# Scores two units ahead in a sparse attention, and a weight's chunks decoded into two separate places

## The chip, the core and the metric

The kernel runs on one core of a Trainium2 chip. The metric is device time in microseconds from the start to the end of one execution; of several executions the median counts. Times inside an execution come from the hardware profiler: PE is the matrix engine (its weight loads are listed apart, as PEld), DVE the vector engine, ACT the scalar engine, POOL the engine for general work, SP the engine whose queue issues most transfers. A queue (SPq, ACTq, POOLq) is the engine's sequencer, which issues DMAs and waits.

## What is computed

Block-sparse attention, followed by a token mix. The attention (batch 4, 8 heads, 768 positions, head width 64) works in 24 blocks of 32 positions. A block of queries sees its own block and both neighbours, the first and the last block, and three blocks drawn at random; the first and the last block see everything.

```python
scores = scale * np.matmul(q, k.transpose(0, 1, 3, 2))
...
scores = np.where(mask, scores, -1000000000.0)
scores = scores - np.max(scores, axis=-1, keepdims=True)
attn = np.exp(scores)
attn = attn / (np.sum(attn, axis=-1, keepdims=True) + 1e-09)
x = np.matmul(attn, v)
...
theta = x @ w_theta
zr, zi = x * np.cos(theta), x * np.sin(theta)
y = np.einsum('ts,bsd->btd', w_tok_r, zr) + np.einsum('ts,bsd->btd', w_tok_i, zi)
u = x + y
out = u + np.maximum(u @ w_ch, 0.0)
```

The weights arrive as 64-bit words and are decoded on the chip into a high and a low part.

## The kernel before

**Units and steps.** The attention has 56 units, 28 for each of two pairs of batches ("pair" 0 and 1). The first six of a pair are edge units (named "w"): the first and the last block of queries against a third of all keys each. The other 22 are inner units, one block of queries each, against 8 gathered blocks of keys. The order of the work is written out by hand: `attention` has one loop over steps n (from line 491), in which each engine gets its instructions in program order. Nothing reorders them, so an instruction that waits holds up all that stand behind it on its engine.

**A unit's chain.** `scores` (line 321): PE multiplies queries and keys into S (line 340, for edge units line 332), and DVE reduces S to the row minima m (line 343; the queries were scaled by -0.125). `weights` (353): four exponentials on ACT make P (line 360). `turn` (364): eight transpositions on PE make T (line 370). `evict` (372): two copies on ACT take T to pT (line 376). `values` (379): PE multiplies pT with the values into X (line 394). `finish` (405): DVE divides by the row sums (lines 401 to 403, or 417), and `store` writes the result to a scratch tensor xs.

**Buffers.** S has two places of two banks, by the unit's parity. T has two banks, both used by each unit. X, P, pT and m have two each; the gathered keys kg and the windows of values va have two, the gathered values vb four.

**One step before.** In step n the order is: decoder's Abs of a new piece (ACT); scores of n+1; a share of the block tables; register loads for n+4; window and sampled keys of n+3 copied into kg (POOL, lines 298 and 277); up to two decoding shares (DVE); turn of n; values of n-1; evict of n; weights of n+1; the third sampled block of n+3 copied (ACT, line 280); queries of n+3 scaled (ACT, line 247); the decoder's copy of the high part (ACT, line 81); finish of n-1; queries of n+6 loaded (SP); values of n+2 gathered (POOL, an indirect DMA, line 314); the window of values of n+1 loaded (SP, line 310), for two units of three after a copy from the other buffer (POOL, line 307); the store of n-1. Keys of pair 1 are loaded in odd steps 5 to 27, two blocks at a time (SP, line 232); its edge queries qe in step 24 (SP, line 258), and they are scaled on ACT in step 25 (line 247).

**Decoding.** A `Piece` is 512 or 576 columns of a weight. It is loaded into one of two raw buffers (line 59, on ACT's queue) and decoded in three shares on DVE: `bits` (lines 68 to 70), `rest` (lines 76 and 78), `low` (lines 85 and 86), with Abs (63) and the high copy (81) on ACT. The loop computes in `due` how many of the shares should be done by step n. Eight "early" pieces (theta and the first half of tok_r) are spread over steps 4 to 28, ten "late" ones (the second half of tok_r, the first two thirds of tok_i) over steps 29 to 52; at most two shares are done in a step. The late ones go to a tile `w_second` that takes the place in which pair 0 had its keys and values, 13824 columns under one tag. What is left of tok_i, and w_ch, are decoded in the token mix.

**The token mix** (`token_mix`, a generator) is advanced by `next(follow)` in the last six steps and then runs to the end: theta, sine and cosine, and the products with tok_r and tok_i (line 672), which are all PE-heavy.

Of the kernel before, what the change touches and what calls it, by code (L numbers as in the profile page):

```python
# [10 lines left out]
F32 = mybir.dt.float32  # L11
F32R = mybir.dt.float32r
# [168 lines left out]
        nc.vector.tensor_scalar(rows[0:96], base, ZEROS, None, op0=ALU.add)  # L181


def attention(tc, qT, qE, kT, vr, sampled, xs, ident, early_pieces, late_pieces, first_place, follow, spares):

# [13 lines left out]
    with ExitStack() as ctx, ExitStack() as early:  # L199
# [20 lines left out]
        def make_places(bp):  # L220

            if bp == 0:
                place = first_place([P, 13824], F32, "kv0")
                k = place[:, 0:6144]
                wide[bp] = [place[:, 6144 + 1040 * c : 6144 + 1040 * (c + 1)] for c in range(6)]
            else:
                k = kp.tile([P, 6144], F32, name="k1")
                wide[bp] = vbs + vbs[:2]
            ks[bp] = k.rearrange("r (s g f) -> r s g f", s=NB, g=8)
# [91 lines left out]
        def scores(unit):  # L321

            bp, i, x = unit
            s = st[unit] = {}
            sc = ps_s[units.index(unit) % 2].tile([P, 2, 2, 256], F32, tag="S", name=f"S{name(unit)}")
            heads = [(b, p, e) for b in range(2) for p in range(4) for e in range(2)]
            if i == "w":
                t, a = x
                q, keys = qes[bp], ks[bp][:, 8 * t : 8 * t + 8]
                for b, s_, e in [(b, p, e) for b, p, e in heads if p < 2]:  # L330
                    rows, p = slice(64 * e, 64 * e + 64), 2 * a + s_
                    nc.tensor.matmul(sc[64 * s_ : 64 * s_ + 64, e, b, :], q[rows, b, p, :], keys[rows, :, 4 * b + p, :], start=True, stop=True)
                if t == 0:
                    mxs[a] = wp.tile([P, 3, 4], F32, tag="mx", name=f"mx{name(unit)}")
                m = mxs[a][:, t]
            else:
                q, keys = qbs.pop((bp, i)), kgs[i % 2]
                for b, p, e in heads:
                    rows = slice(64 * e, 64 * e + 64)
                    nc.tensor.matmul(sc[32 * p : 32 * p + 32, e, b, :], q[rows, b, p, :], keys[rows, :, 4 * b + p, :], start=True, stop=True)  # L340
                m = wp.tile([P, 4], F32, tag="m", name=f"m{name(unit)}", bufs=2)

            nc.vector.tensor_reduce(m.rearrange("r (e b) -> r e b", e=2), sc, axis=AX.X, op=ALU.min)  # L343
# [118 lines left out]
        spares.append(lambda: qp.tile([P, 4, 4, 32], F32, tag="q", name=f"spare{len(spares)}", bufs=Q_BUFS))  # L462
        with tc.manual_schedule():
            load_edges(0)
# [22 lines left out]
            making = tab.make(nc, cp)  # L487
            next(making)
            do(0, weights)
            steps = len(units) + 1  # L490
            for n in range(steps):
                if n == len(units) - 1:
                    early_s.close()
                    next(follow)

                if n <= half:
                    due = 3 * len(early_pieces) * max(n - 3, 0) // (half - 3)
                else:

                    weight = lambda k: 4 * min(k, 6) + 7 * max(k - 6, 0)  # L500
                    due = 3 * len(early_pieces) + 3 * len(late_pieces) * weight(n - half) // weight(len(units) - 4 - half)
                due = min(due, 3 * len(decoder.pieces)) - decoder.at
                decoder.first_on_scalar(due)
                do(n + 1, scores)
                next(making, None)
                inner(n + 4, number_blocks)
                inner(n + 3, gather_window)
                inner(n + 3, gather_keys)
                if due > 0:
                    decoder.on_vector()  # L510
                if due > 1 and decoder.at % 3:
                    decoder.on_vector()
                do(n, turn)
                do(n - 1, values)
                if len(units) - 2 <= n < len(units):
                    next(follow)
                do(n, evict)
                do(n + 1, weights)
                inner(n + 3, gather_key)
                inner(n + 3, scale_q)  # L520
                decoder.on_scalar()
                do(n - 1, finish)
                if units[min(n + 6, steps - 2)][:2] not in ((0, 1), (0, 3)):
                    inner(n + 6, load_q)
                inner(n + 2, gather_values)

                inner(n + 1, lambda bp, i: load_window(bp, i) if i > 2 else None)
                inner(n + 3, lambda bp, i: load_window(bp, i) if i <= 2 else None)
                inner(n - 1, store)

                if n <= len(units) and units[n - 1][1:] in (("w", (2, 0)), ("w", (2, 1))):
                    joins.append(join(units[n - 1][0], units[n - 1][2][1]))
                if n % half > 6 and joins and next(joins[0], joins) is joins:
                    joins.pop(0)
# [12 lines left out]
                if len(units) - 6 <= n < len(units):  # L547
                    next(follow)
# [286 lines left out]
def sparse_attention_then_token_mix(ctx, tc, qT, qE, kT, vr, sampled, w_theta, w_tok_r, w_tok_i, w_ch, outT):  # L835
# [15 lines left out]

    def first_place(shape, dtype, name):
        return const.tile(shape, dtype, tag="place", name=name)

    rest = []

    def second():
        if not rest:  # L860
            rest.append(first_place([P, 2, 9 * 768], F32R, "w_second"))
        return rest[0]

    def tok(at):

        tile_, k = (first, at) if at < 3 else (second(), at - 3)
        return [tile_[:, x, 768 * k : 768 * k + 768] for x in range(2)]

    w["tok_r"] = tok
    w["tok_i"] = lambda j: tok(6 + j)  # L870
# [12 lines left out]

    def chunks(tile_, at, n):
        return lambda: [tile_()[:, x, 768 * at : 768 * (at + n)] for x in range(2)]

    early = pieces("theta", 0, 2048, 512, all_of("theta")) + pieces("tok_r", 0, 2304, 576, chunks(lambda: first, 0, 3))
    late = pieces("tok_r", 2304, 4608, 576, chunks(second, 0, 3)) + pieces("tok_i", 0, 3072, 512, chunks(second, 3, 4))

    def last():  # L890
        return pieces("tok_i", 3072, 4608, 256, chunks(second, 7, 2)) + pieces("ch", 0, 2048, 256, all_of("ch"))

    spares = []
    follow = token_mix(tc, w, last, xs, outT, bias, n_batch, lambda: spares[0]())
    attention(tc, qT, qE, kT, vr, sampled.bitcast(I32), xs, ident, early, late, first_place, follow, spares)
    for _ in follow:
        pass

# [46 lines left out]
```

## Time and profile before

| | us |
|---|---|
| median of 3 executions | 596.28 |
| the three executions | 595.65, 596.28, 603.92 |
| the profiled execution | 599.4 |
| its span, first to last instruction | 597.6 |
| PE busy (matmuls) | 548.1 |
| DVE busy | 423.8 |
| ACT busy | 335.6 |
| POOL busy | 180.8 |

How to read it: the profiled execution is a single one, 3.1 us above the median; its rows are compared with its own time. A row of stretches gives for each engine the busy time and, in brackets, the count of instructions. A row of waits reads "engine, what waited, <- what ended the wait: us in total, times, longest". In a timeline the columns are start, duration, engine, line, operation, output <- inputs, count, and in square brackets the idle time of the engine before it and what ended that. "issue" stands for idle time in which the engine waited for nothing that the profile shows. Durations of matmuls overlap, since they are pipelined. In a row of groups stand busy us and mean ns of one between the bars.

### The profile page before, as it was taken

The numbers are of one execution on the slowest core, as the hardware profiler recorded it, in microseconds if no ns is written. First come the engines' busy times: TensorE is split into PE (matmuls) and PEld (weight loads), VectorE is DVE, ScalarE is ACT, GpSimd is POOL, SyncE is SP. The second block draws the span as 40 slices with busy tenths as digits, with TensorE's granted clock in tenths as the row PEclk, the third lists the DMA queues.
The fourth block names the chain that finished last, engine by engine and source line by source line (L and its number), as shares of the span: only waits on it lengthen the run. The fifth ranks groups of instructions, "written<-read, shape, count | busy, mean of one in ns | idle before, by whom it ended". The sixth has DMA issues, their size and how long they took to land.

```text
span 597.6 us, 17323 instructions
## 1 busy us (share of the span) xinstructions
PE 548.1 (92%) x7092; PEld 436.6 (73%) x7092; DVE 423.8 (71%) x846; ACT 335.6 (56%) x684; POOL 180.8 (30%) x281
## 2 busy tenths in 40 slices
PE   6997886979967878999999999999999999999997
PEld 4765555556645545678888888888888888888886
DVE  3786876977889999968999996557732759613352
ACT  4797876758978866875565653344630445521220
POOL 1387957942687888530010010000000000000000
PEclk9898988979999998899999999999999999999999
DMA  8979889879988996852333132220212311102002
GB/s 313 353 216 263 249 254 258 233 199 318 282 242 236 238 251 184 207 159 73 94 84 104 43 89 88 89 62 10 71 36 79 95 39 34 37 27 81 1 1 105
DMA packets 53087, 86.67 MB, mean 145 GB/s; under 512 B 5392, under 2 KB 31632, under 8 KB 52624
## 3 DMA queue, kind: packets, MB, share of 16 engines
q1 hardware_dynamic: 43200, 53.28, 29.2%
q0 software_dynamic: 6944, 22.85, 14.4%
q10 hardware_dynamic: 2864, 9.44, 5.4%
q8 instruction: 56, 0.92, 0.7%
q14 instruction: 23, 0.19, 0.1%
HBM read 72.95 MB, written 12.58 MB: 143 GB/s over the span
## 4 chain that ended last, share of the span: by engine, by line
PE 36%; DVE 11%; ACT 5%; DMA 2%; issue 1%; DVEq 0%
PE ya L672 14%; PE yb L672 7%; PE o L697 2%; PE o L698 2%; PE o L699 2%; PE h L613 2%; PE h L616 2%; PE h L614 2%; ACT zh L654 2%; ACT t L623 1%; DVE rr L630 1%; DVE rr L629 1%; DVE xT L598 1%; DMA xa<-xs 1%; ACT t L622 1%
## 5 line engine op out<-in xcount | busy, mean ns | idle before, releaser
L672 PE MATMUL ya<-w_second,zh 128*128 128x512 f32 x288 | 106.9, 395 | 0.0
L672 PE MATMUL yb<-w_second,zh 128*128 128x256 f32 x288 | 80.2, 279 | 0.0
L360 ACT ACTIVATE P<-S,m 128x256 f32<-128x256 f32 x176 | 70.0, 499 | 14.9 <-DVE m L343 13.6
L370 PE MATMUL T<-ident,P 128*128 128x128 f32 x352 | 60.7, 301 | 10.0 <-ACT P L360 8.6
L370 PEld LDWEIGHTS T<-ident,P 128*128 128x128 f32 x352 | 41.7, 148 | 36.9 <-ACT P L360 29.6
L672 PEld LDWEIGHTS ya<-w_second,zh 128*128 128x128 f32 x288 | 54.1, 188 | 13.6
L343 DVE TENSOR_REDUCE m<-S 128x4 f32<-128x1024 f32 x44 | 53.6, 1217 | 10.2 <-PE S L340 9.0
L340 PE MATMUL S<-kg,q 64*32 64x256 f32 x1408 | 53.6, 390 | 7.2 <-issue 7.2
L394 PE MATMUL X<-vb,pT 128*32 128x65 f32 (+1 forms) x1408 | 50.4, 230 | 10.2 <-issue 10.1
L376 ACT COPY pT<-T 128x512 f32<-128x512 f32 x88 | 47.9, 601 | 19.4 <-PE T L370 18.9
L394 PE MATMUL X<-va,pT 128*32 128x65 f32 (+1 forms) x1408 | 50.4, 233 | 7.9 <-issue 5.4
L672 PE MATMUL ya<-w_second,zl 128*128 128x512 f32 x144 | 57.6, 400 | 0.0
L672 PEld LDWEIGHTS yb<-w_second,zh 128*128 128x128 f32 x288 | 54.3, 188 | 0.4
L314 POOL DMA_INDIRECT vb<-in_vr_dram,rows x44 | 46.1, 1047 | 20.3 <-PE X_w L394 8.6
L394 PEld LDWEIGHTS X<-va,pT 128*32 128x32 f32 (+1 forms) x1408 | 35.6, 116 | 16.7 <-issue 12.4
L394 PEld LDWEIGHTS X<-vb,pT 128*32 128x32 f32 (+1 forms) x1408 | 37.9, 117 | 12.2 <-issue 12.0
L705 DVE SCALAR_TENSOR_TENSOR of<-o,xT 128x512 f32<-128x512 f32 (+1 forms) x24 | 13.3, 557 | 46.0 <-PE o L699 42.5
L672 PE MATMUL yb<-w_second,zl 128*128 128x256 f32 x144 | 40.6, 282 | 0.0
L307 POOL COPY va<-va 32x1040 f32<-32x1040 f32 (+1 forms) x28 | 31.6, 1129 | 27.8 <-DMA va<-in_vr_dram 20.9
L613 PE MATMUL h<-w_theta_hi,xh 128*128 128x512 f32 x96 | 38.2, 398 | 0.4 <-ACT xh L602 0.4
L340 PEld LDWEIGHTS S<-kg,q 64*32 64x32 f32 x1408 | 23.0, 107 | 20.5 <-issue 11.7
L614 PE MATMUL h<-w_theta_lo,xh 128*128 128x512 f32 x96 | 37.9, 394 | 0.0
(169 smaller groups left out, 1309.2 us busy)
## 6 DMA issues: line engine op xcount, KB each, us to landing
va<-in_vr_dram SPq DMA_DIRECT2D x58, 130.0 KB
q<-in_qT_dram SPq DMA_DIRECT2D x22, 256.0 KB
xs<-xo SPq DMA_DIRECT2D x22, 256.0 KB
xr<-xs SPq DMA_DIRECT2D x22, 256.0 KB
xa<-xs SPq DMA_DIRECT2D x88, 64.0 KB
raw_tok_r<-in_w_tok_r_dram ACTq DMA_DIRECT2D x8, 576.0 KB
out_dram<-of SPq DMA_DIRECT2D x16, 256.0 KB
kv<-in_vr_dram SPq DMA_DIRECT2D x6, 520.0 KB
```

The costliest lines, as they stand in the source:

```text
L307: nc.gpsimd.tensor_copy(va[rows], vas[(i + 1) % 2][rows])
L314: nc.gpsimd.indirect_dma_start(out=vbs[(i + 1) % VB][rows], out_offset=None, in_=vr, in_offset=bass.IndirectOffsetOnAxis(ap=tab.rows[rows, ...
L340: nc.tensor.matmul(sc[32 * p : 32 * p + 32, e, b, :], q[rows, b, p, :], keys[rows, :, 4 * b + p, :], start=True, stop=True)
L343: nc.vector.tensor_reduce(m.rearrange("r (e b) -> r e b", e=2), sc, axis=AX.X, op=ALU.min)
L360: nc.scalar.activation(pt[:, e, b], sc[:, e, b], AF.Exp, bias=m[:, 2 * e + b : 2 * e + b + 1], scale=-1.0)
L370: nc.tensor.transpose(banks[k // 4][:, k % 4], pt[:, (k // 2) % 2, k % 2, 128 * (k // 4) : 128 * (k // 4) + 128], ident)
L376: nc.scalar.copy(out[:, 4 * h : 4 * h + 4], bank)
L394: nc.tensor.matmul(s["X"][rr, b, e, :], s["T"][0:rows, 4 * c + 2 * e + b, rr], v[0:rows, v0 : v0 + 65], start=c == 0, stop=c == 1,)
L613: nc.tensor.matmul(ps, hi[:, c, :], wh[:, c, :], start=c == 0, stop=False)
L614: nc.tensor.matmul(ps, hi[:, c, :], wl[:, c, :], start=False, stop=False)
L672: nc.tensor.matmul(acc, z[:, dd], wt[:, t0 : t0 + n], start=first and (n == 512 or c % 2 == 0), stop=last, skip_group_check=n == 256,)
L705: nc.vector.scalar_tensor_tensor(o, ps, 0.0, xT[b][:, e : e + groups, t0 : t0 + n], op0=ALU.max, op1=ALU.add)
```

## The change

The scores run two units ahead of the transposition instead of one, and stand behind it in the step: turn of n, scores of n+2, values of n-1. On ACT the weights of n+1 stand ahead of the eviction of n. m gets a third buffer. Queries are scaled for n+4 instead of n+3 and loaded for n+7 instead of n+6; pair 1's edge queries are loaded in step 18 instead of 24 and scaled in step 24 instead of 25. The gathers of keys and values keep their steps.

The place of 13824 columns becomes two, keys (6144) and values (7680). The second half of tok_r is decoded into the values' place, the first four chunks of tok_i into the keys' place, and the last two of tok_i into what is left of the values' place. With that one schedule serves all 18 pieces: shares are spread from unit 5 to step 52 with weight 4 for an edge unit and 7 for an inner one.

```diff
-            if bp == 0:
-                place = first_place([P, 13824], F32, "kv0")
-                k = place[:, 0:6144]
-                wide[bp] = [place[:, 6144 + 1040 * c : 6144 + 1040 * (c + 1)] for c in range(6)]
+            if bp == 0:
+                k, v = first_places()
+                wide[bp] = [v[:, 1040 * c : 1040 * (c + 1)] for c in range(6)]
...
-                m = wp.tile([P, 4], F32, tag="m", name=f"m{name(unit)}", bufs=2)
+                m = wp.tile([P, 4], F32, tag="m", name=f"m{name(unit)}", bufs=3)
...
             do(0, weights)
+            do(1, scores)
             steps = len(units) + 1
...
-                if n <= half:
-                    due = 3 * len(early_pieces) * max(n - 3, 0) // (half - 3)
-                else:
-                    weight = lambda k: 4 * min(k, 6) + 7 * max(k - 6, 0)
-                    due = 3 * len(early_pieces) + 3 * len(late_pieces) * weight(n - half) // weight(len(units) - 4 - half)
+                weight = lambda k: sum(4 if u[1] == "w" else 7 for u in units[5:k])
+                due = 3 * len(decoder.pieces) * weight(n) // weight(len(units) - 4)
                 due = min(due, 3 * len(decoder.pieces)) - decoder.at
                 decoder.first_on_scalar(due)
-                do(n + 1, scores)
+                do(n, turn)
+                do(n + 2, scores)
                 next(making, None)
                 inner(n + 4, number_blocks)
                 inner(n + 3, gather_window)
...
-                do(n, turn)
                 do(n - 1, values)
                 if len(units) - 2 <= n < len(units):
                     next(follow)
+                do(n + 1, weights)
                 do(n, evict)
-                do(n + 1, weights)
                 inner(n + 3, gather_key)
-                inner(n + 3, scale_q)
+                inner(n + 4, scale_q)
                 decoder.on_scalar()
                 do(n - 1, finish)
-                if units[min(n + 6, steps - 2)][:2] not in ((0, 1), (0, 3)):
-                    inner(n + 6, load_q)
+                if units[min(n + 7, steps - 2)][:2] not in ((0, 1), (0, 3)):
+                    inner(n + 7, load_q)
...
-                if n == 24:
+                if n == 18:
                     load_edges(1)
-                if n == half - 3:
+                if n == half - 4:
                     scale_edges(1)
...
+    def first_places():
+        return const.tile([P, 6144], F32, tag="keys", name="k0"), const.tile([P, 7680], F32, tag="values", name="v0")
...
+    def of_keys():
+        return second("keys", 6144).rearrange("r (x f) -> r x f", x=2)
+
+    def of_values(part):
+        f0, f1 = ((0, 4608), (4608, 7680))[part]
+        return second("values", 7680)[:, f0:f1].rearrange("r (x f) -> r x f", x=2)
...
+    w["tok_r"] = lambda j: chunk(first, j) if j < 3 else chunk(of_values(0), j - 3)
+    w["tok_i"] = lambda j: chunk(of_keys(), j) if j < 4 else chunk(of_values(1), j - 4)
...
-    late = pieces("tok_r", 2304, 4608, 576, chunks(second, 0, 3)) + pieces("tok_i", 0, 3072, 512, chunks(second, 3, 4))
+    late = pieces("tok_r", 2304, 4608, 576, both(lambda: of_values(0))) + pieces("tok_i", 0, 3072, 512, both(of_keys))
```

More of the change, by code (lines that the diff above doesn't have):

```diff
@@ L181, in make, with attention @@
         nc.vector.tensor_scalar(rows[0:96], base, ZEROS, None, op0=ALU.add)
-def attention(tc, qT, qE, kT, vr, sampled, xs, ident, early_pieces, late_pieces, first_place, follow, spares):
+def attention(tc, qT, qE, kT, vr, sampled, xs, ident, early_pieces, late_pieces, first_places, follow, spares):
     nc = tc.nc
@@ L850, in sparse_attention_then_token_mix, with second, chunk @@
     words = {n: a.bitcast(I32) for n, a in dict(theta=w_theta, tok_r=w_tok_r, tok_i=w_tok_i, ch=w_ch).items()}
[L854 to L866, printed above, removed]
+    def first_places():
+        return const.tile([P, 6144], F32, tag="keys", name="k0"), const.tile([P, 7680], F32, tag="values", name="v0")
+    rest = {}
+    def second(tag, size):
+        if tag not in rest:
+            rest[tag] = const.tile([P, size], F32R, tag=tag, name=f"w_{tag}")
+        return rest[tag]
+    def of_keys():
[3 more added lines that the diff above has]
+        return second("values", 7680)[:, f0:f1].rearrange("r (x f) -> r x f", x=2)
+    def chunk(tile_, k):
         return [tile_[:, x, 768 * k : 768 * k + 768] for x in range(2)]
-    w["tok_r"] = tok
-    w["tok_i"] = lambda j: tok(6 + j)
+    w["tok_r"] = lambda j: chunk(first, j) if j < 3 else chunk(of_values(0), j - 3)
+    w["tok_i"] = lambda j: chunk(of_keys(), j) if j < 4 else chunk(of_values(1), j - 4)
     def pieces(name, f0, f1, f, tiles):
@@ L882, in all_of, with both @@
         return lambda: [t.rearrange("p c f -> p (c f)") for t in w[name]]
-    def chunks(tile_, at, n):
-        return lambda: [tile_()[:, x, 768 * at : 768 * (at + n)] for x in range(2)]
-    early = pieces("theta", 0, 2048, 512, all_of("theta")) + pieces("tok_r", 0, 2304, 576, chunks(lambda: first, 0, 3))
-    late = pieces("tok_r", 2304, 4608, 576, chunks(second, 0, 3)) + pieces("tok_i", 0, 3072, 512, chunks(second, 3, 4))
+    def both(tile_):
+        return lambda: [tile_()[:, x] for x in range(2)]
+    early = pieces("theta", 0, 2048, 512, all_of("theta")) + pieces("tok_r", 0, 2304, 576, both(lambda: first))
+    late = pieces("tok_r", 2304, 4608, 576, both(lambda: of_values(0))) + pieces("tok_i", 0, 3072, 512, both(of_keys))
     def last():
-        return pieces("tok_i", 3072, 4608, 256, chunks(second, 7, 2)) + pieces("ch", 0, 2048, 256, all_of("ch"))
+        return pieces("tok_i", 3072, 4608, 256, both(lambda: of_values(1))) + pieces("ch", 0, 2048, 256, all_of("ch"))
     spares = []
     follow = token_mix(tc, w, last, xs, outT, bias, n_batch, lambda: spares[0]())
-    attention(tc, qT, qE, kT, vr, sampled.bitcast(I32), xs, ident, early, late, first_place, follow, spares)
+    attention(tc, qT, qE, kT, vr, sampled.bitcast(I32), xs, ident, early, late, first_places, follow, spares)
     for _ in follow:
```

## The prediction

> **What bounds the kernel now.** I read the page first, then the busy time by stretches, the waits of each stretch, and the timelines of PE, ACT, DVE and POOL around the longest waits. The stretches cut at 28, 121, 146, 248 and 265 us separate the inner units of the first head pair, the edge units of the second, its inner units, the handover, and the token mix.
>
> ```profile
> span 597.6 us, 17323 instructions
> 28.00:121.00 93.00, 77.19 (x2148) 53.81 (x2144) 72.98 (x132) 73.34 (x174) 72.64 (x109) 0.94 0.87 244
> 121.00:146.00 25.00, 21.85 (x418) 15.06 (x416) 18.63 (x33) 17.64 (x40) 8.56 (x14) 0.86 0.90 263
> 146.00:248.00 102.00, 82.47 (x2241) 56.85 (x2240) 94.91 (x161) 79.94 (x187) 76.69 (x110) 0.97 0.89 239
> 265.00:598.00 333.00, 327.61 (x1783) 281.24 (x1781) 208.27 (x442) 135.57 (x224) 6.49 (x12) 1.00 0.20 63
> ```
>
> The columns are stretch, length, busy us of PE, PE weight loads, DVE, ACT and POOL, then granted clock, DMA share and GB/s. After 265 us PE is busy for 327.61 of 333 us, and the change leaves that work as it is: what can move lies before 265. There three things stand close together. The DMA engines are 87 to 90% busy all the time. In the second pair DVE is busy for 94.91 of 102 us (93%); in the first it is at 72.98 of 93 (78%). And PE has holes of two kinds, which the waits of both stretches show (first pair, then second):
>
> ```profile
> POOL va L307 <- DMA va<-in_vr_dram: 7.7, 4, 2.8
> PEld T L370 <- ACT P L360: 9.5, 25, 1.4
> ...
> PEld T L370 <- ACT P L360: 16.2, 31, 2.7
> ACT P L360 <- DVE m L343: 10.9, 8, 2.8
> POOL va L307 <- DMA va<-in_vr_dram: 6.7, 4, 2.4
> ```
>
> The first kind is the transposition T waiting for the exponentials P: 9.5 and 16.2 us. It is a loop: scores, reduction on DVE, exponentials on ACT, transposition, all with one unit of lead. In the second pair the late link is named: ACT waits 10.9 us for the reduction m, which on DVE stands behind decoding. The second kind has no operand to wait for:
>
> ```profile
> 28.53 0.84 PE L340 MATMUL S<-kg,q 64*32 64x256 f32 x19
> ...
> 63.25 1.09 PE L340 MATMUL S<-kg,q 64*32 64x256 f32 x32
> 64.28 1.09 PE L370 MATMUL T<-ident,P 128*128 128x128 f32 x8
> 65.30 0.32 PE L394 MATMUL X<-va,pT 128*32 128x65 f32 x8
> 66.34 1.09 PE L340 MATMUL S<-kg,q 64*32 64x256 f32 x32
> ...
> 91.13 0.31 PE L394 MATMUL X<-vb,pT 128*32 128x65 f32 x5
> 94.58 0.32 PE L394 MATMUL X<-vb,pT 128*32 128x65 f32 x2 [3.14 <-issue]
> ...
> 120.96 1.09 PE L340 MATMUL S<-kg,q 64*32 64x256 f32 x32
> PE X L394 <- issue: 15.5, 12, 3.1
> PE S L340 <- issue: 7.2, 5, 2.5
> q8 instruction: 56, 0.92, 0.7%
> ```
>
> An unhindered step takes 66.34 - 63.25 = 3.09 us; the 21 steps from 28.53 to 120.96 took 4.40 each. The hole at 94.58 falls inside one run of like matmuls; from 28 to 248 us such holes make 15.5 + 7.2 = 22.7 us. Queue 8 brings the instructions: 0.92 MB in 56 packets, 16.4 KB each, and PE's 2 x 7092 matmuls and weight loads are 253 to a packet, a packet every 1.2 steps. I read the holes as PE having used up a packet before the next came through busy DMA engines: at a DMA share of 0.20 (265 to 598) they are gone. That is an inference; no row names it.
>
> **The change, part by part.**
>
> *Scores two ahead, exponentials ahead of the eviction.* No instruction is added. PE's order in a step becomes T(n), S(n+2), X(n-1); ACT's becomes exponentials (n+1), eviction (n). T(n) then needs P(n), which ACT made in the step before from scores a whole step older, so the 9.5 + 16.2 us lose their cause. Scores n+2 go into the score bank of unit n, whose reader, the exponentials of n, ran a step earlier; the third buffer of m covers the third unit in flight. The eviction of n now stands behind 1.57 us of exponentials on ACT, but T(n) is first on PE, and X(n) comes a full step later.
>
> What is late next differs by pair. *First pair:* DVE takes on work and stays below 90% (below), so the instruction packets decide. PE sees somewhat less than one hole in two packets (12 + 5 from 28 to 248 us, in which the stretch rows count 9607 matmuls and weight loads, or 38 packets). A PE that reaches the end of a packet 1 us sooner waits up to 1 us longer if that packet is late, and gains the whole 1 us if it is not. I take half of 9.5: **-4.7**, between 0 and -9.5.
>
> The Trainium skill, "Runtime: NRT & Kernel Launch", section "Instruction fetch mechanics", says that the sequencer streams the program in 16 KiB blocks through a DMA queue of its own and that crossing a block's edge is mostly hidden. The block's size agrees with the 16.4 KB here; hidden it is from 265 us on, but not in the 22.7 us of holes. By the page all 9.5 us would be gained; that is a rival below.
>
> *Second pair:* DVE is the floor, and the other half of the change lowers it.
>
> *One schedule, places split.* The decoder's 54 shares ran 24 up to step 28 and 30 after it. With weights 4 and 7 from unit 5 on, step 28 stands at 54 x 158 // 308 = 27: three shares, one piece, leave the second pair. tok_r's later chunks can go into the values' place because step 6 reads that last; the keys' place is first written at share 36, about step 37, long after its last gather at step 24. A piece costs, in the second pair (six pieces) and in the first (four of theta):
>
> ```profile
> 146.00:248.00 102.00, 28.76 (x36) 7.96 (x12) 0.97 0.89 239
> L78 DVE SCALAR_TENSOR_TENSOR raw_tok_i<-raw_tok_i,ds_tok_i 128x512 f32<-128x512 uint32 x6 | 6.2, 1030 | 0.2
> 28.00:121.00 93.00, 15.13 (x24) 5.69 (x8) 0.94 0.87 244
> L78 DVE SCALAR_TENSOR_TENSOR raw_theta<-raw_theta,ds_theta 128x512 f32<-128x512 uint32 x4 | 2.9, 730 | 0.1
> ```
>
> The stretch rows are those of the tiles da_tok_i and da_theta, DVE first. (28.76 + 6.2) / 6 = 5.8 us a piece late, (15.13 + 2.9) / 4 = 4.5 us early. So DVE in the second pair falls to 94.9 - 5.8 = 89.1 us; at the 93% that it reaches now, the stretch takes 89.1 / 0.93 = 95.8: **-6.2**. With no idle time on DVE it would be -12.9; if DVE stretches its operations as the stretch gets shorter, 0. That happens already: this DVE operation takes 2.76 us beside POOL's copies and 0.69 us at 234.68.
>
> ```profile
> 224.23 2.76 DVE L86 TENSOR_TENSOR w_second<-da_tok_i,raw_tok_i 128x512 fp32r<-128x512 f32 x1
> 234.68 0.69 DVE L86 TENSOR_TENSOR w_second<-da_tok_i,raw_tok_i 128x512 fp32r<-128x512 f32 x1
> ```
>
> In the first pair 73.0 + 5.8 = 78.8 of 88 us stays off the bound (90%); if that cover goes, it costs what the second pair shows, up to 5.8. The piece's packets move with it (0.5 MB, 2 us at 244 GB/s), which makes the first pair's DMA tighter; it is inside the halving above.
>
> *Edge queries of the second pair, loaded at step 18 instead of 24 and multiplied at 24 instead of 25.* Now the load is issued at 120.83 and ACT stands still for it, with everything behind it on ACT: Abs of a piece, eviction, exponentials.
>
> ```profile
> 120.83 0.42 SPq L258 DMA_DIRECT2D qe<-in_qE_dram  x1
> 126.98 0.63 ACT L247 ACTIVATE qe<-qe 128x512 f32<-128x512 f32 x1 [4.32 <-DMA qe<-in_qE_dram]
> 127.67 1.70 PE L332 MATMUL S_w<-k,qe 64*64 64x256 f32 x16 [2.77 <-ACT qe L247]
> 129.62 2.42 PE L370 MATMUL T<-ident,P 128*128 128x128 f32 x8 [0.26 <-ACT P L360]
> ```
>
> With six steps of lead the transfer lies under other work. PE loses 2.77 us, and 2.42 instead of 1.09 us in the next T, at a clock of 0.86 over this stretch. I take **-4**, between -2.8 and -6.
>
> *Gathers and queues.* load_q and its scaling run one step earlier and change no count: 22 loads, 256 KB each. SP's queue gets load_q(n+7) where n+6 stood, with the tile it overwrites used two steps before; load_edges passes the key loads of steps 18 to 24. What shrinks is POOL's lead: the keys of unit n+3 are still copied in step n, but now read in step n+1, not n+2. POOL runs in order, and ahead of those copies stands the copy of va, which waits for a DMA:
>
> ```profile
> 192.35 1.04 POOL L307 COPY va<-va 32x1040 f32<-32x1040 f32 x1 [2.40 <-DMA va<-in_vr_dram]
> 193.35 0.60 POOL L298 COPY kg<-k 128x512 f32<-128x512 f32 x1
> 193.90 1.67 POOL L277 COPY kg<-k 128x256 f32 x2
> L307 POOL COPY va<-va 32x1040 f32<-32x1040 f32 (+1 forms) x28 | 31.6, 1129 | 27.8 <-DMA va<-in_vr_dram 20.9
> vb<-in_vr_dram,rows POOLq DMA_INDIRECT x44, 6.1
> ```
>
> From the end of X(n-1) POOL needs 1.04 + 0.60 + 1.67 = 3.3 us, and the scores come after one step and a T: 3.09 + 1.02 = 4.1 us later. So 0.8 us of lateness is hidden at full pace, 2 us at today's 4.4 us a step. The eight waits of 7.7 + 6.7 = 14.4 us average 1.8. I take **+2**, between 0 and +14.4.
>
> *Start and end* I cost at nothing: up to 28.53 us PE works on edge units, whose scores wait for the first key loads, and these keep their order; the last transpositions alternate with theta matmuls of the token mix. If that fails it is 1 us either way.
>
> **Sum.** -4.7 - 6.2 - 4 + 2 = -12.9 us. The profiled execution took 599.4 us (span 597.6 and 1.8 around it), so 586.5 on its terms; it stands 3.1 above the median of 596.28, and against that median I forecast **583.4 us**.
>
> **Rivals.**
>
> 1. *The packets and the DMA hold the pace* (0.22). PE only runs sooner into the next hole; DMA shares of 0.87 to 0.90 speak for it, the 10.9 us that ACT demonstrably waits for DVE speaks against. What remains is the edge queries: 596.3 - 4 = 592.
> 2. *Everything is covered* (0.14). Packets arrive early enough once PE no longer works in bursts, and DVE runs without idle time: -9.5 - 12.9 - 4 = -26.4, 570. The 22.7 us of holes speak against it. The rule of the Trainium skill cited above ("Runtime: NRT & Kernel Launch") comes to this in the first pair.
> 3. *POOL becomes the loop, and the kernel slower* (0.08). A va load is issued at the end of X(n-2), lands, is copied, then keys are copied, and now the scores two steps and a T later need them: landing + 3.3 <= 2 steps + 1.02. With the 6.1 us of the indirect load as landing, a step must be at least 4.2 us, harmless. At 8 us it must be 5.1, against 4.4 now: 28 steps with such a copy x 0.7 = +20, less the 4 of the edge queries: 612. It decides from a landing of 6.6 us. For it: 8 of 28 copies wait already; against: 6.1.
> 4. *The lead isn't kept* (0.06): scores n+2 find their keys late often enough that T waits as before, about 596.
>
> **Numbers.** The forecast has 0.50. About half of it lies below 584.4, the bound of 2% (596.28 x 0.98), which is about what a measurement can tell here: 0.28 with rival 2's 0.14 and a little of rival 4's spread make 0.43 faster. Slower by over 2% (above 608.2) is rival 3, 0.08. The rest, 0.49, lies within. The range goes from 571, all but the full cover, to 597, where nothing is gained. The forecast's own range is 576 to 590.
>
> **What would show it.** Right: T's wait for P below 5 us over both pairs; ACT's for m near 0; no wait for qe; the second pair's stretch near 96 us with DVE still at 93% or more; holes of "issue" at 22.7 us or above. Wrong: a wait of S for POOL's or ACT's kg above 5 us in all (rivals 3 and 4), the stretches unchanged with "issue" up by about 20 us (rival 1), or a first pair near 83 us (rival 2).

## The result, and the profile after

The changed kernel is slower: 619.41 us median of 4 runs (617.96 to 629.58) against 600.10 for the kernel before on the same chip, a ratio of 1.033 with a 95% interval of 1.026 to 1.040. The profiled execution took 617.96 us with a span of 616.2. The prediction's sum, made against 599.4, said -12.9; it became +18.6. The kernel before had medians of 601 to 605 us beside the experiments below, so each kernel is compared by its ratio to the runs of before that stand beside it; ratios leave out runs in the slower state of a chip, those more than 1.5% above the fastest of their kernel.

The stretches (columns as in the prediction) answer to those of before:

```profile
28.00:121.00 93.00, 69.43 (x1872) 48.86 (x1872) 73.62 (x118) 66.03 (x158) 70.38 (x104) 0.91 0.83 230
121.00:146.00 25.00, 18.83 (x476) 13.21 (x461) 19.61 (x38) 15.99 (x39) 10.36 (x11) 0.79 0.70 201
146.00:248.00 102.00, 78.42 (x2047) 55.27 (x2053) 82.34 (x139) 74.73 (x178) 68.79 (x103) 0.93 0.75 227
```

Every engine gets through less in the first and in the third stretch: PE 1872 matmuls where it did 2148, and 2047 where it did 2241. No engine comes clearly nearer to full than before (DVE is busy for 73.62 of 93 us, where it was 72.98, and for 82.34 of 102, where it was 94.91), and the DMA share fell to 0.75 in the third. When everyone does less, a loop of waits is the first suspicion. PE's groups name it; the last column is the idle time of PE just before the group, and what ended it:

```profile
L369 PE MATMUL T<-ident,P 128*128 128x128 f32 x352 | 54.6, 303 | 37.3 <-ACT pT L375 37.3
L339 PE MATMUL S<-kg,q 64*32 64x256 f32 x1408 | 59.0, 434 | 6.4 <-POOL kg L276 4.0 <-issue 2.4
```

The same two groups of the kernel before (lines are one higher there):

```profile
L370 PE MATMUL T<-ident,P 128*128 128x128 f32 x352 | 60.7, 301 | 10.0 <-ACT P L360 8.6
L340 PE MATMUL S<-kg,q 64*32 64x256 f32 x1408 | 53.6, 390 | 7.2 <-issue 7.2
```

So the waits of T for P went, as forecast, and 37.3 us of T waiting for pT came: T(n+1) writes the two banks that ACT's eviction of n (L375, it reads T and writes pT) has to empty first. One such wait in order of time, from the timeline of the changed kernel (start, length, engine; idle time in brackets):

```profile
72.93 1.09 PE L339 MATMUL S<-kg,q 64*32 64x256 f32 x32
74.56 0.98 DVE L86 TENSOR_TENSOR w_theta_lo<-da_theta,raw_theta 128x512 fp32r<-128x512 f32 x1
75.62 0.34 ACTq L59 DMA_DIRECT2D raw_tok_r<-in_w_tok_r_dram  x1
76.00 0.66 ACT L63 ACTIVATE da_theta<-raw_theta 128x512 f32<-128x512 f32 x1 [3.40 <-issue]
76.57 1.55 ACT L359 ACTIVATE P<-S,m 128x256 f32<-128x256 f32 x4
77.99 1.09 ACT L375 COPY pT<-T 128x512 f32<-128x512 f32 x2
78.64 1.15 PE L369 MATMUL T<-ident,P 128*128 128x128 f32 x8 [3.57 <-ACT pT L375]
79.72 1.59 PE L339 MATMUL S<-kg,q 64*32 64x256 f32 x32
```

Read it from below. T waits 3.57 us for the eviction; that stands behind the exponentials, these behind Abs, and Abs behind a raw load on ACT's queue, which is issued at 75.62, just after DVE's last operation on the piece two earlier (L86) ended at 75.54; the load takes that piece's raw buffer. ACT works in the order of the program: its compute stood idle for 3.40 us behind a load that has nothing to do with exponentials or eviction. What the trace alone can't say is which link has to be loosened.

### The profile page after: what moved, and what is told of

Same layout as the page of the kernel before. It is cut to its first block, busy times and chain, and to the rows that moved or that the text cites. A ratio compares the mean times of both kernels' runs of the same rounds, so it can differ in the third digit from the quotient of the medians.

```text
span 616.2 us, 17363 instructions
## 1 busy us (share of the span) xinstructions
PE 547.1 (89%) x7092; PEld 437.6 (71%) x7092; DVE 429.3 (70%) x846; ACT 333.0 (54%) x684; POOL 183.4 (30%) x281
## 4 chain that ended last, share of the span: by engine, by line
PE 67%; DVE 10%; ACT 7%; issue 7%; DMA 6%; POOL 2%; SPq 1%; ACTq 1%; POOLq 0%; DVEq 0%
PE ya L670 22%; PE yb L670 11%; PE S L339 4%; PE h L611 4%; PE h L614 3%; PE h L612 3%; PE T L369 3%; DMA va<-in_vr_dram 3%; ACT P L359 3%; PE o L695 3%; PE o L696 3%; PE o L697 3%; PE X L393 2%; DVE m L342 2%; ACT pT L375 2%
## 5 line engine op out<-in xcount | busy, mean ns | idle before, releaser
L369 PE MATMUL T<-ident,P 128*128 128x128 f32 x352 | 54.6, 303 | 37.3 <-ACT pT L375 37.3
L359 ACT ACTIVATE P<-S,m 128x256 f32<-128x256 f32 x176 | 69.3, 488 | 0.7 <-DVE m L342 0.6
L339 PE MATMUL S<-kg,q 64*32 64x256 f32 x1408 | 59.0, 434 | 6.4 <-POOL kg L276 4.0
L670 PE MATMUL ya<-w_values,zh 128*128 128x512 f32 x160 | 59.4, 395 | 0.0
L313 POOL DMA_INDIRECT vb<-in_vr_dram,rows x44 | 44.7, 1015 | 25.2 <-PE X_w L393 13.0
L375 ACT COPY pT<-T 128x512 f32<-128x512 f32 x88 | 48.6, 626 | 0.0
L670 PE MATMUL ya<-w_keys,zh 128*128 128x512 f32 x128 | 47.6, 396 | 0.0
L276 POOL COPY kg<-k 128x256 f32 x88 | 46.0, 550 | 0.0
L297 POOL COPY kg<-k 128x256 f32<-128x256 f32 (+2 forms) x66 | 37.3, 584 | 28.3 <-DMA k<-in_kT_dram 18.1
L306 POOL COPY va<-va 32x1040 f32<-32x1040 f32 (+1 forms) x28 | 31.8, 1137 | 44.3 <-DMA va<-in_vr_dram 21.1
L670 PE MATMUL yb<-w_values,zh 128*128 128x256 f32 x160 | 44.6, 278 | 0.0
L627 DVE SCALAR_TENSOR_TENSOR rr<-t,h 128x512 f32<-128x512 f32 x24 | 16.5, 687 | 29.3 <-ACT t L621 29.3
```

What stands on the lines that cost most here:

```text
L276: nc.gpsimd.tensor_copy(*sampled_keys(bp, i, k))
L297: nc.gpsimd.tensor_copy(kgs[i % 2][:, s0 : s0 + n], ks[bp][:, b0 : b0 + n])
L313: nc.gpsimd.indirect_dma_start(out=vbs[(i + 1) % VB][rows], out_offset=None, in_=vr, in_offset=bass.IndirectOffsetOnAxis(ap=tab.rows[rows, ...
L359: nc.scalar.activation(pt[:, e, b], sc[:, e, b], AF.Exp, bias=m[:, 2 * e + b : 2 * e + b + 1], scale=-1.0)
L369: nc.tensor.transpose(banks[k // 4][:, k % 4], pt[:, (k // 2) % 2, k % 2, 128 * (k // 4) : 128 * (k // 4) + 128], ident)
L375: nc.scalar.copy(out[:, 4 * h : 4 * h + 4], bank)
```

## The experiments

### Is it the schedule, or the edge queries?

**e3_lead_only**: the changed kernel with the due times of before. **e4_schedule_only**: the kernel before with the two places and one schedule. **e7_edges_only**: the kernel before with

```
-                if n == 24:
+                if n == 18:
                     load_edges(1)
-                if n == half - 3:
+                if n == half - 4:
                     scale_edges(1)
```

> The changed kernel with the old schedule of the shares (24 up to step 28, 30 after); order, lead, places and edge queries as changed. Theory C (the schedule is the loss): 585 to 600. Theories A and B (the order is the loss): still 18 pieces whose load holds ACT, 610 to 622.

> The kernel before with the two places and the one schedule alone: order, lead, queries and edge queries as before. My forecast's second half was worth 6 us (one piece leaves the second pair): 590 to 600. Theory C: slower than before, 608 or more. Theory A: ACT is not ahead of DVE in this order, so the loads wait little, and it is within 8 us of the kernel before.

> The kernel before with the second pair's edge queries loaded at step 18 in place of 24 and scaled one step earlier, nothing else. The prediction's term: the wait of the scale for qe, 4 us, goes and the time falls by 4 us, ratio 0.990 to 0.996. Rival: the wait goes, and VectorE's decoding, which went on meanwhile, has less of a lead afterwards, so the time stays within 0.3%.

e3: 620.26 us, ratio 1.036 (1.032 to 1.040): the loss stays without the new schedule. e4: 599.70 us, 0.999 (0.993 to 1.004), and e7: 601.35 us, 1.000 (0.996 to 1.004): the other two parts are worth nothing that can be seen, where the prediction had -6.2 and -4. So the loss is in the reordering of the units. In e7 pair 1's wait for qe is gone, so PE's wait of 2.77 us did go, and the time did not follow.

### Is it the decoding?

**e8_lead_no_decode** and **e9_before_no_decode**: the changed kernel and the one before, each without loading and decoding the pieces inside the attention; DVE fills their places with zeros.

> The changed kernel without decoding in the attention: the 18 pieces are neither loaded nor decoded (their places are filled with zeros by DVE), so ACT has no work that waits for DVE's shares. To be read against the same cut in the kernel before, run beside it. A2: with no tie the lead is worth something, 5 to 20 us less than that one. D: the lead costs even so, equal or more.

> The kernel before with the same cut: no piece is loaded or decoded in the attention. Less DVE work, 9 MB less to load: 555 to 590 by any theory; what counts is the difference to the changed kernel with the same cut.

e8: 573.94 us, 0.952 (0.942 to 0.962); e9: 572.92 us, 0.951 (0.942 to 0.960). Two things follow. Without the decoding the lead costs nothing, so the loss needs the decoding; no wait of T for pT is left in e8. (e8 leaves out the pieces' transfers and most of DVE's part as well, so it does not say which part of the decoding matters.) And without it the lead brings nothing either, as theory D said: the loop that the change was said to relieve isn't worth anything once the decoding is gone.

### Which tie of ScalarE?

**e1_raw_on_sp** moves the raw loads to SP's queue (`Decoder(early_pieces + late_pieces, stage, nc.sync)`). **e2_evict_first** puts eviction of n ahead of the exponentials of n+1. **e6_high_behind** puts the high copy of a piece (L81) behind the next step's eviction, **e5_decoder_behind** that and the load with Abs as well. The edit of e5 ("..." marks lines left out):

```
-                decoder.first_on_scalar(due)
                 do(n, turn)
...
-                if due > 0:
-                    decoder.on_vector()
-                if due > 1 and decoder.at % 3:
-                    decoder.on_vector()
                 do(n - 1, values)
...
                 do(n, evict)
                 inner(n + 3, gather_key)
+                decoder.on_scalar()
+                decoder.first_on_scalar(due)
+                if due > 0:
+                    decoder.on_vector()
+                if due > 1 and decoder.at % 3:
+                    decoder.on_vector()
                 inner(n + 4, scale_q)
-                decoder.on_scalar()
```

> The changed kernel with one edit: the raw pieces are loaded from SP's queue and not from ACT's. Theory A: the 37 us for which the transposition now waits for pT come from ACT's queue. There the load of raw piece k+2 stands at the head of the step and waits until DVE has decoded piece k, and Abs, the exponentials and the eviction stand behind it; the next transposition needs the banks which that eviction frees. On SP the load stands behind a store that waits for a later DVE instruction anyway, so nothing new waits. A expects T's waits for pT below 10 us and a time of 580 to 598, at or below the kernel before. Theory B (the eviction is late because it stands behind the exponentials) and theory C (the uniform schedule puts too much decoding into the first pair) expect no change: 614 to 622.

> The changed kernel with the eviction of n ahead of the exponentials of n+1 on ACT again, as before the change; the scores stay two ahead. Theory B: the eviction comes 1.45 us earlier in each step, T's waits for pT go, and the time falls to 585 to 600. Theory A: the next transposition needs both, the exponentials and the freed banks, and both stand behind the load of a raw piece, so T waits as long for P as it did for pT: 612 to 622.

> The other single edit beside the raw load on SP: the high copy alone goes behind, to the step after its bits, while the raw load and Abs stay at the head of ACT's step. A2: one of the two ties is left, T still waits 25 to 40 us for pT, 608 to 620. If 600 or less, the high copy was the whole of it.

> The raw load on SP only moved the wait: ACT then stood 59 us for the bits of a piece, ahead of the copy of its high part. New theory A2: ACT is tied to DVE at two places of each piece, the raw load with Abs at the head of a step and the high copy at its end, and exponentials and eviction stand behind both. Here both go behind: in a step ACT runs exponentials (n+1), eviction (n), the third key block, then the high copy of the piece whose bits were made in the step before, the raw load and Abs; DVE's order stays. A2 expects T's waits for pT below 12 us and a time of 580 to 600. Theory D (the lead itself costs: kg copied too late, two T banks, holes of issue) expects 612 to 622 still, with T's waits or S's waits for kg above 25 us.

e1: 620.13 us, 1.037 (1.027 to 1.047). The theory that the load alone does it falls; ACT now waits at the next tie, the high copy for its bits:

```profile
PEld T L369 <- ACT pT L375: 41.3, 20, 6.1
...
ACT w_keys L81 <- DVE da_tok_i L70: 23.0, 6, 5.9
...
ACT w_values L81 <- DVE da_tok_r L70: 15.2, 4, 4.9
ACT w_first L81 <- DVE da_tok_r L70: 13.7, 4, 5.0
```

e2: 623.47 us, 1.044 (1.040 to 1.047); T now waits 30.1 us for P in place of pT, so the two orders on ACT only exchange the operand that is late. e6: 614.88 us, 1.021 (1.012 to 1.031), an interval that overlaps that of the changed kernel, and T's waits for pT are longer, 43.3 us. e5: 607.82 us, 1.008 (1.004 to 1.012), with T's waits for pT down to 19.1 us in 14 places (in a profiled execution of 613.27 us). That is between the two forecasts. Moving both ties takes most of the loss away; moving the load alone changes nothing (e1), and moving the high copy alone nothing that is clear of the noise (e6). In e1 the other tie takes over, as the rows above show.

### Which order on TensorE?

Theory A2 put it on PE's side: with T(n) ahead of S(n+2), PE has too little work beside the loop. **e10_scores_first** exchanges two calls:

```
-                do(n, turn)
                 do(n + 2, scores)
+                do(n, turn)
```

**e11_three_banks** gives T three banks and X one (`ps_t` bufs 3, `ps_x` bufs 1). **e12_behind_scores_first** is e5 with e10's exchange.

> The changed kernel with one pair of calls exchanged: S(n+2) stands ahead of T(n) on TensorE instead of behind it; lead, schedule and ScalarE's order stay. Theory A2 (the loop S, minimum, decoding, ScalarE's load and Abs, exponentials, eviction, next T has too little TensorE work beside it, 5.15 us a turn where it takes 7.1 to 9.1): with S first the same loop has two whole steps and an S beside it, about 7.2 us as before the change, so the waits of T for pT fall from about 40 us to under 15 and the time to 598 to 607. Rival B (it is ScalarE's two ties to the decoding alone, and where S stands among TensorE's work does not matter, since VectorE takes its minimum when the decoding lets it): waits of T for pT stay over 30 us, time 614 to 621.

> The changed kernel with three banks for T in place of two, and one for X in place of two, nothing else. Theory A2 (T(n+1) waits because both of T's banks are freed by the eviction of n, which is late): the first half of T(n+1) no longer waits for that eviction, so its waits fall by 0.7 to 1.2 us in each of 18 places, 12 to 20 us of 40, and the time to 600 to 608, less what X now loses waiting for VectorE to finish the sums of the unit before (a new wait of X for sm or xo, 0 to 15 us). Rival B (the banks are not what T waits for in effect; what is late is late for the whole step): T waits as long for its second half, time 615 to 622.

> Both remedies together: ScalarE's load, Abs and high copy behind exponentials and eviction as in e5_decoder_behind (607.8 us), and S(n+2) ahead of T(n). Theory A2: what was left of the waits of T for pT there (17 us) falls under 6 and the time to 592 to 602, at or just under the kernel before. Rival C (with the ties behind, the exponentials' wait for the minimum, 40 us there, sets the pace and stays since VectorE is what is late): waits of P for m stay over 30 us and the time at 604 to 610.

e10: 616.92 us, 1.029 (1.021 to 1.036). Neither forecast held whole. The waits for pT are all gone, as A2 said, and the time stayed, as its rival said:

```profile
L339 PE MATMUL S<-kg,q 64*32 64x256 f32 x1408 | 58.7, 426 | 42.3 <-POOL kg L276 14.3 <-issue 10.8 <-POOL kg L297 6.8
L369 PE MATMUL T<-ident,P 128*128 128x128 f32 x352 | 54.9, 306 | 0.0
```

S, which now comes first, waits for its keys instead. The change left the copies of unit n+3's keys in step n, and their scores had moved to step n+1. Of the three sampled key blocks two are POOL's, with the window, and the third is ACT's (L279), and that one stands directly behind the eviction. One step of e10:

```profile
77.11 1.09 ACT L375 COPY pT<-T 128x512 f32<-128x512 f32 x2
78.05 0.46 ACT L279 COPY kg<-k 128x256 f32 x1
78.60 1.10 PE L339 MATMUL S<-kg,q 64*32 64x256 f32 x32 [1.73 <-issue]
79.63 1.09 PE L369 MATMUL T<-ident,P 128*128 128x128 f32 x8
```

S starts 0.09 us after ACT's copy ends at 78.51, though its wait has no releaser in the row. In this step S waits for the same late end of ACT's step for which T had waited; in others POOL's copies are named, 14.3 + 6.8 = 21.1 of the 42.3 us. e12: 620.01 us, 1.034 (1.027 to 1.042), worse than e5, with 23.6 us of S waiting for kg. e11: 620.39 us, 1.036 (1.028 to 1.043):

```profile
L369 PE MATMUL T<-ident,P 128*128 128x128 f32 x352 | 56.5, 300 | 2.0 <-issue 0.8
PE X L393 <- issue: 41.3, 35, 4.0
```

With the third bank T's wait is gone, and in 25 of 55 units T starts before ACT has ended the first copy of the eviction before it, by up to 1.22 us; in the changed kernel it never does. So it is the banks that T waits for. The wait came back as one of X, which lost a buffer in this run: of its 21 waits over 0.7 us, 16, with 33.7 us in all, end within 0.1 us of DVE's L402, which reads that one buffer. What free banks alone would be worth therefore stays open.

### Both loops at once

The keys can be copied one unit earlier without another buffer, since S(n+2) has just read the one that n+4 will use:

```
-                inner(n + 4, number_blocks)
-                inner(n + 3, gather_window)
-                inner(n + 3, gather_keys)
+                inner(n + 5, number_blocks)
+                inner(n + 4, gather_window)
+                inner(n + 4, gather_keys)
...
-                inner(n + 3, gather_key)
+                inner(n + 4, gather_key)
```

**e15_keys_early** is the changed kernel with this, **e13_first_keys_early** e10 with this, **e14_all_three** e12 with this.

> The changed kernel with the keys one unit earlier, T still ahead of S. Theory D: S's 4 us of waits for kg go, those of T for pT (37 us) stay, time 613 to 619. Rival F (ScalarE is late at the eviction because its own key copy waits for S and stands ahead of the high copy and the exponentials): T's waits fall under 20 us, time 600 to 608.

> e10 (S ahead of T, 616.9 us) with the keys' block numbers and copies one unit earlier (n+4 in place of n+3 in step n; the buffer is that which S(n+2) has just read). Theory D (two tight loops: T's banks by way of ScalarE's eviction, and the keys, which POOL copies at n+3 while the scores moved to n+2): S's waits for kg fall from 27.5 us to under 8, no other wait takes them over, time 592 to 604. Rival E (POOL and ScalarE are late for what stands ahead of the copies, the values' copies with their transfers and the decoding, so the wait moves): S or X waits 20 us or more for something else, time 610 to 618.

> e12 (S first, and ScalarE's load, Abs and high copy behind exponentials and eviction, 620.0 us) with the keys one unit earlier. Theory D: S's waits for kg fall from 29.7 us to under 8, time 590 to 602, no more than e13's. Rival E: the 25 us come back as waits of X for va or of P for m, time 612 to 620.

e13: 601.18 us, 0.996 (0.991 to 1.001): the loss is gone. e15: 610.07 us, 1.011 (1.006 to 1.015), better than theory D said though T's waits hardly fell; it is outside both forecasts. e14: 606.11 us, 1.003 (1.000 to 1.006): with both loops loose, holding ACT's decoding back brings nothing more. ACT waits 23.7 us for m, and what PE feels is X's wait for va's transfer, 22.0 us against 5.3 in e13; why the transfer comes later was not traced. PE's groups, e15 first, then e13:

```profile
L339 PE MATMUL S<-kg,q 64*32 64x256 f32 x1408 | 56.3, 424 | 1.5 <-issue 1.4
L369 PE MATMUL T<-ident,P 128*128 128x128 f32 x352 | 55.1, 304 | 36.9 <-ACT pT L375 32.5 <-issue 2.8 <-ACT pT_w L375 1.4
```

```profile
L339 PE MATMUL S<-kg,q 64*32 64x256 f32 x1408 | 60.4, 402 | 14.9 <-issue 13.6 <-POOL kg L276 0.7 <-POOL xw_w L427 0.3
...
L369 PE MATMUL T<-ident,P 128*128 128x128 f32 x352 | 50.8, 289 | 1.4 <-issue 1.4
```

PE's idle time before the inner units' T, S and X, in us (X is the sum of its two groups, for va and vb):

| kernel | order on PE | keys copied at | idle before T + S + X | profiled span | ratio |
|---|---|---|---|---|---|
| before | S, T | n+3, scored two steps on | 10.0 + 7.2 + 18.1 = 35.3 | 597.6 | 1 |
| changed | T, S | n+3, scored one step on | 37.3 + 6.4 + 10.6 = 54.3 | 616.2 | 1.033 |
| e10 | S, T | n+3 | 0.0 + 42.3 + 8.0 = 50.3 | 612.5 | 1.029 |
| e15 | T, S | n+4 | 36.9 + 1.5 + 13.3 = 51.7 | 610.2 | 1.011 |
| e13 | S, T | n+4 | 1.4 + 14.9 + 21.3 = 37.6 | 597.6 | 0.996 |

Only both edits together take the idle time back to about that of before. The changed kernel has 19.0 us more of it than before and a span 18.6 us longer, e10 15.0 and 14.9. e15 does not fit: 16.4 us more idle time, but a span only 12.6 us longer. T still waits 36.9 us there, and the ratio is 1.011; why that wait costs so much less than its length stays open.

### Is there anything to gain?

**e16_and_raw_on_sp** is e13 with the raw loads on SP's queue, **e17_high_behind_too** that with e6's edit, **e18_e16_again** the kernel of e16 once more.

> e13 with the raw pieces loaded by SP's queue in place of ScalarE's. Theory G (ScalarE's tie keeps the gain away): its 13 us of waits for issue go, the time falls under e13's, 588 to 597, ratio to before 0.975 to 0.992. Rival H (TensorE's holes without a releaser, 28 of its 44.5 us of idle time, and the transfers set what is left; a raw load on SP that waits for the decoding holds the values' loads behind it): the ratio stays within 0.993 to 1.010 and POOL's waits for va's transfer grow past 19 us.

> e16 with the high copy of a piece behind the exponentials and the eviction of the next step. Theory G (what is left hangs on ScalarE's ties to the decoding): ScalarE's 26 us of waits for the bits no longer stand ahead of exponentials, time 588 to 595, ratio 0.973 to 0.987. Rival I (as in e14, an order in which the decoding comes later on VectorE is paid back in waits of the exponentials for the minimum): ratio 0.995 to 1.010.

> e16 unchanged, measured again. If the gain is one: ratio 0.983 to 0.996 with an interval that ends below 1. If it was scatter: 0.996 to 1.004.

e16: 598.50 us, 0.990 (0.980 to 0.999); the ratio is in theory G's range, the interval reaches into H's. e18, the same kernel: 599.94 us, 0.996 (0.992 to 1.000), on the border between its two forecasts. e17: 598.79 us, 0.996 (0.992 to 1.000), as rival I said. The intervals end at 1 or just below it. If there is a gain, it is about half a percent; one of 1% or more lies outside the intervals of e17 and e18, and only e16's allows it.

## Why the prediction was wrong

Two terms of the sum failed: the new order on PE, which was put at nothing, and POOL's shorter lead, which was put at +2.

**The new order.** The first step that failed is "The eviction of n now stands behind 1.57 us of exponentials on ACT, but T(n) is first on PE, and X(n) comes a full step later", which costed the new order at nothing. It followed the eviction's result to its reader X(n) and not its source, T's two banks, to their next writer, T(n+1), which the change had made first on PE. That wait was 37.3 us. That T waits for the banks is what e11 shows. That the wait hangs on the new order together with the decoding is shown in two ways: S ahead of T ends it (e10, e13), and so does leaving the decoding out (e8). That the eviction is late because ACT waits for DVE's decoding at two places, the load with Abs and the high copy, is what e5 shows; e1 and e6 show that neither alone carries it. The price of the order is smaller than the wait: 1.011 - 0.996 = 1.5% with the keys early (e15 against e13), 9 us of 600, and 1.033 - 1.029 = 0.4% with the keys late (the changed kernel against e10), which is within the noise.

**POOL's shorter lead** was seen and mis-sized: +2, with an upper end of 14.4, from the waits of POOL for va. The runs put the keys' late copies at 1.033 - 1.011 = 2.2% with T first (e15), 13 us of 600, and at 1.029 - 0.996 = 3.3% with S first (e13 against e10), 20 us. So this term, not T's 37.3 us, was the dearer of the two. The working looked at POOL alone; the third key block's copy on ACT, behind the eviction, was not in it. Its sign of being wrong, a wait of S for kg above 5 us, did not show either: the row had 4.0 us while T, first in the step, waited 37.3; with S first (e10) it is 21.1 us for POOL's copies alone. The third rival, a loop by way of POOL to 612 us, was in place nearest to what happened, though it took only the one engine; the landing from which it was said to decide is 6.5 us by its own sum (2 x 4.40 + 1.02 - 3.31), not 6.6. How the 20 us divide between POOL's two copies and ACT's one stays open: no run moved them apart.

**T's wait for P**: right that it goes (10.0 us before, nothing in the row above), right that ACT no longer waits for m (0.7 us before P in the changed kernel's groups). Wrong in its size: the 9.5 and 16.2 us are rows of PEld, the weight loads, which can wait while earlier matmuls still run. PE's matmuls themselves waited for P for 1.3 us in the first pair, and in the second for

```profile
PE T L370 <- ACT P L360: 6.7, 4, 2.2
```

So the 4.7 us of the first pair were not there to be gained. In e13, where T waits 1.4 us in all, S and X wait longer instead (the table above), and the ratio is 0.996.

**DVE as the floor of the second pair**, -6.2: e4 took the same piece out of the pair and gained nothing. In the changed kernel DVE did 139 instructions in that stretch where it had done 161. Whether the 93% was a limit at all stays open: the kernel before gains 4.9% when the decoding is left out (e9), but that frees ACT and the transfers too.

**The edge queries**, -4: e7 gives 0, with an interval of 2.6 us either way. What took the place of PE's 2.77 us was not traced.

**The holes of "issue"**: forecast at 22.7 us or above. With T stalled they were fewer: PE's row of issue for X fell from 15.5 us to 8.7, that for S from 7.2 to 2.4. In e13 the rows have 12.2 and 13.6. But three of S's waits there, 3.37, 2.33 and 1.16 us, end 0.10 us after ACT's exponentials (L359) of unit n, which read the banks that S(n+2) writes: these 6.9 us are ACT's lateness once more and no hole. What is left, 18.9 us, is less than the 22.7 before. e13's 0.996 is close to the first rival's 592 on 596.28 (0.993), but whether instruction packets make the holes stays unproven; no run changed the packets.

## What to carry over

When a unit is brought forward, follow every buffer both ways, to its next writer as well as its reader, and bring forward by the same count each copy that feeds it, on every engine that makes one. When a wait of 37 us is undone and the time stays, look for the operand that was late behind it: if two operands come from the end of the same in-order step, changing the order only changes the name of the wait, and what an edit is worth depends on the other (0.4% and 1.5% here for the order on PE). Read the waits of the matmuls, not those of their weight loads. A compute engine whose queue also issues loads is tied to whatever frees their buffers.

## What the runs showed of the hardware

A wait of PE of more than 3 us cost more than itself here. After the 3.57 us wait in the timeline above T took 1.15 us, but the next S 1.59 us where an S at full pace takes 1.09. In e13, after a wait of 3.37 us, S and the next T took nearly double:

```profile
71.86 1.56 ACT L359 ACTIVATE P<-S,m 128x256 f32<-128x256 f32 x4
73.52 1.96 PE L339 MATMUL S<-kg,q 64*32 64x256 f32 x32 [3.37 <-issue]
75.41 1.97 PE L369 MATMUL T<-ident,P 128*128 128x128 f32 x8
79.38 1.09 PE L339 MATMUL S<-kg,q 64*32 64x256 f32 x32
80.41 1.09 PE L369 MATMUL T<-ident,P 128*128 128x128 f32 x8
```

The granted clock of e13 was 0.50 from 73.50 to 77.40 us and 1.00 from 79.40 to 82.00. By stretches, it was 0.79 from 121 to 146 us in the changed kernel, where PE was busy for 18.83 of 25 us, and 0.86 before, where PE was busy for 21.85. The Trainium skill, "TensorE: Matmul & The Clock Gate", section "Part 1: The HAM clock gate (the "warmup" mystery)", has the clock fall to half after an idle window of about 3.4 us, until a window as long has been busy. The 1.96 and 1.97 us against 1.09, and 1.09 again some 6 us after the wait, agree with that. So this one wait also cost 0.87 us on S and 0.88 us on T; what shorter waits cost in clock was not measured.

The profile's releaser is not always the operand that was late: e10's S at 78.60 began 0.09 us after ACT's key copy, and the S of e13 at 73.52 began 0.10 us after the exponentials in the first row above, and both rows say "issue".
